# Local and global attention feeding a two-matrix feed-forward: maxima moved behind other VectorE work, low words moved to GpSimd

## The chip, the cores and the metric

One core of a Trainium2 chip. The metric is device microseconds of one execution, as the median of several runs; lower is better. The engines are PE (TensorE, matmuls), DVE (VectorE), ACT (ScalarE), POOL (GpSimd) and SP (which issues the DMAs). Each engine works through its own instructions in order; an instruction whose input is not ready holds back all that stand behind it on that engine.

## What is computed

```
k_all, v_all = concat(k_g, k_l), concat(v_g, v_l)      # batch 8, heads 8, 32 global + 512 local, depth 64
out_g = softmax(scale * q_g @ k_all.T) @ v_all
s_l   = concat(scale * q_l @ k_g.T, where(|i - j| <= 32, scale * q_l @ k_l.T, -1e9))
out_l = softmax(s_l) @ v_all
x = concat(out_g, out_l) as (4352 tokens, 512)
h = x @ w_in                                           # 512 x 2048
out = (h * cos(h)) @ w_out                             # 2048 x 512
```

Inputs and output are float32. w_in and w_out arrive as 64-bit words.

## The kernel before, in words

Matmuls run in 16-bit pairs: a float32 operand is split into a high plane and a low plane (float16), and three products (high x high, high x low, low x high) are summed. To split, an operand is first scaled by a power of two, which takes its maximum: of v for each batch (`v_a`), of w_in (`w_in_max`, `w_in_max_done`, `w_in_done`) and of w_out (`w_out_max`, `w_out_done`).

**Attention** runs in 32 groups: 8 batches b, two halves h of the queries, two groups g of two head pairs p. For a pair and half, `sc_a` computes scores (L549), `sc_b` adds the mask and takes the row minimum of the negated scores on DVE (L602), `sc_c` takes Exp on ACT (L437), `sc_d` normalizes into planes (L656, L657), `sc_e` transposes them (L679 by DMA, in the first half by PE and copies), `av_a` multiplies with the planes of v (L721), `av_b` scales the result by `xs` into x's high plane on ACT (L743) and low plane on DVE (L744). `g_a` and `g_b` compute the global queries' scores (L763, from batch 3 on L772) and minima (L785). `load_v` brings v of a batch into one buffer (L453); `v_a` takes its maximum on DVE (L488), `v_d` makes its planes.

**Feed-forward** runs in 17 chunks of 256 tokens (two to a batch; the last holds the global tokens) of 8 steps j. `m1_a` multiplies x with two 128-column blocks of w_in into a PSUM tile `ph` of three (L896); `m1_b` reduces the phase on ACT and DVE (L919, L920), `m1_c` takes Sin on ACT (L437), `m1_d` forms gf on DVE (L936), its high plane gh on ACT (L940) and low plane gl on POOL (L247); gf frees `ph`. `m2_a` multiplies gh, gl with w_out three steps later (L966). Exp and Sin need different ACT tables; `table_act` keeps them in the order in which they are written.

**Weights.** w_in comes in 8 blocks k (pair kc = k // 2, even or odd half of the columns): `w_in_load`, `w_in_max` (L280 on DVE), and `w_in_piece`: `decode` scales the high words on ACT (L261), makes the low words on DVE (L262) and joins both on DVE (L266); `split_w` casts to the high plane on ACT (L273), and POOL subtracts for the low plane (L247). Odd blocks lie raw in the tile that later holds w_out's planes, `wo_hl`. `xs`, the scale of x, needs the maxima of all of w_in. w_out comes in 16 blocks: each is loaded once for its maximum (`w_out_max`: the load at L406 and the reduction at L280 in one step, in borrowed room named by `ROOM`), and once more for its decoding (`w_out_load` for the first eight, or inside `w_out_piece`). `w_out_done` turns the maxima into the scale `wsc`.

**Order.** `at(slot, phase, f, ...)` writes the steps into slots, by hand; a step of the feed-forward takes slot 8c + j, and an attention group n has its parts at fixed distances from slot t = 4n + T0. Each step gets a priority from `pr` (or its own slot and phase), and a scheduler with a timeline simulation orders the instructions of each engine by priority among those that are ready in it. `behind(ins, what)` adds an order without a semaphore: the instruction is placed behind another. Line L1073 ff. set w_in's and w_out's steps, L1085 ff. the groups:

```
at(WOE + k // WOS, PJ, w_out_max, k, pr=(WO + k // WOS, PI))
...
at(-9, PB, w_out_done, pr=(WO + 7, PI))
...
t = 4 * n + T0
```

Of the kernel before, what the change touches and what calls it, by code (L numbers as in the profile page):

```python
# [49 lines left out]
LGC = 2  # L50
ROOM = "hlhlrrqqhlhlrrqq"
GB = 4
# [22 lines left out]
SW = 256  # L75
LO = "m01v456789:;"
JA = [None, "xl3", None, "xl3", None, "xl3", None, "xl3"]
# [69 lines left out]
def body(tc, qf, v, wi, wo, mask, out):  # L147
# [3 lines left out]
    with ExitStack() as ctx:  # L151
# [25 lines left out]

        wi_h = cp.tile([P, NPAIR, DF], F16, name="wi_h")
        wi_l = cp.tile([P, NPAIR, DF], F16, name="wi_l")
        wo_hl = cp.tile([P, NJ, 2, DM], F16, name="wo_hl")  # L180
# [76 lines left out]

        def decode(y, raw, s, low_after=None, join_after=None):
# [12 lines left out]

        def split_w(h, l, z, on_vector=False, cast="A", n=SPLIT):
            {"A": nc.scalar.copy, "D": nc.vector.tensor_copy, "G": nc.gpsimd.tensor_copy}[cast](h, z)  # L273
            if on_vector:
                nc.vector.tensor_tensor(l, z, h, op=ALU.subtract)
            else:
                pool_tt(l, z, h, ALU.subtract, n)

        def raw_max(o, raw):
# [45 lines left out]
        def w_in_max(k):  # L325
# [5 lines left out]
            if k % 2:  # L331
                m = wim[:, kc : kc + 1]
                nc.vector.tensor_reduce(m, wfs["s", kc], axis=AX.X, op=ALU.max)
                s = w1.tile([P, 1], F32, tag="ws", name=f"ws_{kc}", bufs=2)
# [61 lines left out]

        def w_out_max(j):
            room = ROOM[j]
            if room == "r":
                raw = w2.tile([P, 1024], U32, tag="raw", name=f"raw_wm{j}")  # L400
            elif room == "q":
                raw = ap_.tile([P, 2 * QK], U32, tag="qkr", name=f"raw_wm{j}", bufs=KQB)[:, :1024]
            else:
                t = ap_.tile([P, NPAIR, SL], F16, tag="x" + room, name=f"raw_wm{j}")
                raw = t.rearrange("p a b -> p (a b)").bitcast(U32)
            ld = nc.sync.dma_start(raw.bitcast(I64), wo[j * P : (j + 1) * P])  # L406
            maxes["wo", j] = raw_max(wos[:, j : j + 1], raw)

        def w_out_piece(j):
            if j < 8:  # L410
                raw = wo_raw[:, j]
# [64 lines left out]
        def v_a(b):  # L476
# [111 lines left out]
        def sc_b(b, p, i):  # L588
# [12 lines left out]
            for h in range(2):  # L601
                nc.vector.tensor_tensor_reduce(  # L602
                    t[:, h], pt[h], msk[:, MOFF[i] : MOFF[i] + w], nal, 3.0e38,
                    ALU.add, ALU.min, mn[:, h : h + 1],
                )
            st["t", b, p, i] = (t, mn)

        def sc_c(b, p, i):
# [6 lines left out]
            for h in range(2):  # L615
                table_act(
                    "Exp", t[:, h], t[:, h], AF.Exp, bias=mn[:, h : h + 1], scale=-1.0,
                    accum_out=sm[:, k + h : k + h + 1],
                )

        def sc_r(rr):
# [3 lines left out]
        def sc_d(b, p, i):  # L625
# [25 lines left out]
            else:  # L651
                for h in range(2):
# [81 lines left out]
        def av_b(b, hf, p):  # L734
            if (hf, p) == (0, 0):
                st["x", b] = (
                    ap_.tile([P, NPAIR, SL], F16, tag="xh", name=f"xh_{b}"),
                    ap_.tile([P, NPAIR, SL], F16, tag="xl", name=f"xl_{b}"),
                )
            xh, xl = (x[:, p, hf * CT : hf * CT + CT] for x in st["x", b])  # L740
# [144 lines left out]
        def m1_a(c, j, part=None):  # L885
# [6 lines left out]
            for a, kc in todo:  # L892
                f = slice((2 * j + a) * P, (2 * j + a + 1) * P)
                first, last = (a, kc) == (0, 0), (a, kc) == (1, NPAIR - 1)
                for ip, (w, x) in enumerate(((wi_h, xh), (wi_h, xl), (wi_l, xh))):
                    nc.tensor.matmul(  # L896
                        ph[:, a], w[:, kc, f], x[:, kc, q],
                        start=first and ip == 0, stop=last and ip == 2, skip_group_check=True,
# [31 lines left out]
        def m1_d(c, j):  # L930
            w = st.pop(("u", c, j))[1]
            n = w.shape[-1]
            gh = mp.tile([P, n], F16, tag="gh", name=f"gh_{c}_{j}", bufs=GB)
            gl = mp.tile([P, n], F16, tag="gl", name=f"gl_{c}_{j}", bufs=GB)
            gf = gf_tile(c, j, n)
# [274 lines left out]
```

## Time and profile before

| what | value |
|---|---|
| median of 3 runs | 947.88 us (945.82 to 949.18) |
| profiled execution, its own time | 949.29 us |
| its span, first to last instruction | 947.5 us |
| mean granted TensorE clock | 0.98 of full speed |
| PE busy | 881.5 us (93%) |
| ACT busy | 716.4 us (76%) |
| DVE busy | 649.5 us (69%) |
| POOL busy | 324.7 us (34%) |
| DMA moved | 104.88 MB, 111 GB/s on average |

The profile is of one execution; its own time is the span and 1.79 us around it. Times in the rows are microseconds from the start of the span. A matmul's record can overlap the one before it, since matmuls are pipelined, so that a busy PE is not PE at its peak. An engine's idle time costs nothing where another engine sets the pace.

### The profile page before, as it was taken

What the parts mean: (1) busy time and instruction counts of PE and PEld (TensorE: products, weight loads), DVE (VectorE), ACT (ScalarE), POOL (GpSimd) and SP (SyncE); (2) the same over time, 40 slices, a digit from 0 to 9 for tenths busy, and PEclk for the clock granted to TensorE, in tenths of its full rate; (3) what the DMA queues carried; (4) which work ended last, traced back from release to release, by engine and by line L of the source; (5) the groups of instructions that cost most, each with busy time, mean ns of one, the idle gap of its engine ahead of it and who ended that gap; (6) DMA issues with size and microseconds to landing.
All of it is one profiled execution on the core that took longest, in us unless ns stands there. A gap on an engine that the chain in (4) does not pass through costs nothing.

```text
span 947.5 us, 21219 instructions
## 1 busy us (share of the span) xinstructions
PE 881.5 (93%) x8055; PEld 594.9 (63%) x8055; DVE 649.5 (69%) x1757; ACT 716.4 (76%) x1472; POOL 324.7 (34%) x670
## 2 busy tenths in 40 slices
PE   5558899999999998999799998999899999999998
PEld 3446565566666665666566665666566676666676
DVE  5998879356766867687677867786777866764321
ACT  6948988678678886888588876898688788875442
POOL 5874556233323221223223322322132422333232
PEclk9997999999999999999899998999999999999999
DMA  9978565254435444433434464454334322430000
GB/s 383 403 268 262 99 169 145 69 107 82 130 75 111 89 105 113 93 92 76 130 62 103 80 148 79 89 98 83 113 75 110 60 68 46 82 59 24 1 24 23
DMA packets 164519, 104.88 MB, mean 111 GB/s; under 512 B 149568, under 2 KB 149952, under 8 KB 162368
## 3 DMA queue, kind: packets, MB, share of 16 engines
q1 hardware_dynamic: 164416, 103.52, 43.1%
q8 instruction: 63, 1.03, 0.5%
q14 instruction: 40, 0.33, 0.1%
HBM read 57.88 MB, written 8.91 MB: 70 GB/s over the span
## 4 chain that ended last, share of the span: by engine, by line
PE 39%; ACT 25%; DVE 24%; DMA 6%; issue 5%; POOL 1%; SPq 0%; ACTq 0%; DVEq 0%; POOLq 0%
PE po L966 18%; PE ph L896 17%; ACT t L437 5%; ACT L437 4%; ACT planes L656 4%; DMA vr<-v 4%; DVE t L602 3%; DVE u L920 3%; ACT w L437 3%; DVE qkr L584 3%; ACT u L919 3%; ACT qh L583 2%; DVE planes L657 2%; PE ps L549 2%; DVE vm L488 2%
## 5 line engine op out<-in xcount | busy, mean ns | idle before, releaser
L247 POOL TENSOR_TENSOR gl<-gf,gh 128x128 f16<-128x128 f32 x544 | 233.6, 463 | 469.7 <-ACT gh L940 431.4
L966 PE MATMUL po<-wo_hl,gh 128*128 128x512 f16 (+1 forms) x1120 | 322.7, 374 | 6.2 <-POOL wo_hl L247 6.2
L896 PE MATMUL ph<-xh,wi_h 128*128 128x256 f16 x1024 | 283.4, 278 | 6.9 <-ACT xh L743 5.2
L896 PE MATMUL ph<-xl,wi_h 128*128 128x256 f16 x1024 | 282.5, 277 | 1.4 <-DVE xl L744 1.4
L896 PE MATMUL ph<-xh,wi_l 128*128 128x256 f16 x1024 | 282.2, 277 | 0.0
L896 PEld LDWEIGHTS <-wi_h 128*128 128x128 f16 x2176 | 209.7, 99 | 54.5 <-issue 18.3
L966 PE MATMUL po<-wo_hl,gl 128*128 128x512 f16 (+1 forms) x560 | 204.6, 375 | 0.0
L966 PEld LDWEIGHTS <-gh 128*128 128x128 f16 x1120 | 109.9, 98 | 101.0 <-issue 2.2
L936 DVE SCALAR_TENSOR_TENSOR gf<-w,ph 128x512 f32<-128x512 f32 x136 | 93.2, 686 | 98.9 <-ACT w L437 97.0
L437 ACT ACTIVATE w<-u,pvs_hp,cs 128x512 f32<-128x512 f32 x136 | 109.9, 812 | 55.1 <-DVE u L920 53.6
L437 ACT ACTIVATE t<-t,mn 128x192 f32<-128x192 f32 (+1 forms) x256 | 116.6, 456 | 35.8 <-DVE mn L602 35.2
L920 DVE SCALAR_TENSOR_TENSOR u<-u,cs,ph 128x512 f32<-128x512 int32 x136 | 101.1, 745 | 58.0 <-ACT u L919 57.9
L919 ACT ACTIVATE u<-ph,pvs_hp,cs 128x512 int32<-128x512 f32 x136 | 104.6, 770 | 26.3 <-PE ph L896 26.3
L896 PEld LDWEIGHTS <-wi_l 128*128 128x128 f16 x1088 | 108.1, 99 | 17.1 <-issue 2.3
L940 ACT CAST gh<-gf 128x512 f16<-128x512 f32 x136 | 83.0, 611 | 37.6 <-DVE gf L936 33.1
L966 PEld LDWEIGHTS <-gl 128*128 128x128 f16 x560 | 54.9, 98 | 68.3 <-issue 7.4
L657 DVE SCALAR_TENSOR_TENSOR planes<-t,sm,planes 128x224 f16<-128x224 f32 (+1 forms) x244 | 93.9, 448 | 0.0
L656 ACT ACTIVATE planes<-t,sm 128x224 f16<-128x224 f32 (+1 forms) x244 | 90.8, 453 | 0.0
L437 ACT ACT_TABLE_LOAD x60 | 77.0, 1283 | 1.8 <-PEq L1200 0.7
L602 DVE CUSTOM_DVE_ANT_0 t<-ps,msk,qs 128x192 f32<-128x192 f32 (+1 forms) x160 | 59.7, 429 | 0.0
L721 PE MATMUL acc<-pt,vh 128*64 128x128 f16 (+2 forms) x896 | 45.7, 227 | 14.4 <-ACT vh L518 4.7
L721 PEld LDWEIGHTS <-vh 128*64 128x64 f16 x896 | 37.5, 113 | 28.9 <-issue 22.9
(176 smaller groups left out, 1066.1 us busy)
## 6 DMA issues: line engine op xcount, KB each, us to landing
qkr<-qf SPq DMA_DIRECT2D x32, 672.0 KB, 4.0
vr<-v SPq DMA_DIRECT2D x8, 1280.0 KB, 6.6
out<-o SPq DMA_DIRECT2D x33, 256.0 KB, 2.5
raw_wm<-wo SPq DMA_DIRECT2D x16, 512.0 KB, 9.8
raw_wi<-wi SPq DMA_DIRECT2D x4, 1024.0 KB, 16.7
wo_hl<-wi SPq DMA_DIRECT2D x4, 1024.0 KB, 18.5
wo_hl<-wo SPq DMA_DIRECT2D x8, 512.0 KB, 6.8
raw_wo<-wo SPq DMA_DIRECT2D x8, 512.0 KB, 4.9
```

The lines of the kernel that those rows point to most:

```text
L247: nc.gpsimd.tensor_tensor(o[..., c], a[..., c], b[..., c], op=op)
L437: ins = nc.scalar.activation(*a, **k).ins
L602: nc.vector.tensor_tensor_reduce(t[:, h], pt[h], msk[:, MOFF[i] : MOFF[i] + w], nal, 3.0e38, ALU.add, ALU.min, mn[:, h : h + 1],)
L656: a = nc.scalar.activation(hi, t[:, h], AF.Identity, scale=r)
L657: d = nc.vector.scalar_tensor_tensor(lo, t[:, h], r, hi, op0=ALU.mult, op1=ALU.subtract)
L721: mm = nc.tensor.matmul(acc[64 * h : 64 * h + 64, q_out : q_out + n0 * len(segs)], vt[:, tl, 64 * h : 64 * h + 64], rhs, start=(k == 0 and ...
L896: nc.tensor.matmul(ph[:, a], w[:, kc, f], x[:, kc, q], start=first and ip == 0, stop=last and ip == 2, skip_group_check=True,)
L919: nc.scalar.activation(k, ph, AF.Identity, scale=st["cs", c][4], bias=quarter)
L920: nc.vector.scalar_tensor_tensor(u, k, m, ph, op0=ALU.mult, op1=ALU.subtract)
L936: nc.vector.scalar_tensor_tensor(gf, w, -0.5, st.pop(("ph", c, j)).rearrange("p a b -> p (a b)"), op0=ALU.mult, op1=ALU.mult,)
L940: nc.scalar.copy(gh, gf)
L966: mm = nc.tensor.matmul(po[n], g[:, a * CT + k * P : a * CT + (k + 1) * P], w[:, 2 * j + a, c0:c1], start=(j == 0 and i == 0), stop=(j == ...
```

## The change

- The maximum of v (batch 1 and later) is placed behind the last score minimum written before it.
- `w_out_max` is divided: `w_out_room` loads a block into borrowed room, `w_out_max` reduces it. Blocks 0 to 11 are loaded right behind the opening's other loads, 12 and 13 at slot -9, 14 and 15 once 8 and 9 have been read. The rooms: both `raw` tiles, two `qkr` buffers, the two buffers each of x's planes, the second halves of `wi_h` and `wi_l` (blocks 8 to 11, then 14 and 15), two `pt` tiles. Maxima 4 and 5 are placed behind `xs`, the other fourteen behind x's low plane of the first half (`xl3`). Blocks 0 to 3 stay and are decoded where they are, without a second load.
- The low words of odd w_in blocks and of all w_out blocks are made by POOL, with a float multiply and add that rounds in place of shift and or.
- `wi_h` and `wi_l` are laid out in two halves by columns. Scaling of odd w_in blocks is placed behind the cast of block 6.
- The scores' operands of batch 0's second half are loaded in the opening (`LO`); its first group runs three slots earlier (`EARLY`); its Exp (i = 2) is placed behind x's high plane `xh3`.
- In chunk 0, gh and gl of steps 4 to 7 lie in batch 1's x tiles, which are taken with batch 0's. The order of the low score planes behind `dx` is gone.

```
+EARLY = {2: 3}
+PLW = "DGDGDGDG"
+PLO = "GGGGGGGGGGGGGGGG"
-ROOM = "hlhlrrqqhlhlrrqq"
+ROOM = "rrqqhlhl0123pp01"
-LO = "m01v456789:;"
+LO = "m01v456789:;23"
...
-            nc.scalar.activation(y, hi, AF.Prelu, scale=s, alpha=2.0**32)
-            low = nc.vector.tensor_scalar(
-                lo, lo, 29, 1, op0=ALU.logical_shift_right, op1=ALU.bitwise_or
-            )
+            p = nc.scalar.activation(y, hi, AF.Prelu, scale=s, alpha=2.0**32)
+            behind(p.ins, scale_after)
+            if pool_low:
+                low = nc.gpsimd.tensor_scalar(lo, lo, 2.0**-29, -0.53125, op0=ALU.mult, op1=ALU.add)
+            else:
+                low = nc.vector.tensor_scalar(
+                    lo, lo, 29, 1, op0=ALU.logical_shift_right, op1=ALU.bitwise_or
+                )
...
-            decode(z, raw, wfs["s", kc], join_after=JA[k])
-            c = slice(k % 2 * 1024, k % 2 * 1024 + 1024)
-            split_w(wi_h[:, kc, c], wi_l[:, kc, c], z, n=WIS)
+            decode(z, raw, wfs["s", kc], join_after=JA[k], pool_low=PLW[k] == "G",
+                   scale_after="cast6" if k % 2 else None)
+            cast = split_w(wi_h[:, k % 2, kc], wi_l[:, k % 2, kc], z, n=WIS)
+            if k == 6:
+                st["cast6"] = cast
...
-            ld = nc.sync.dma_start(raw.bitcast(I64), wo[j * P : (j + 1) * P])
-            maxes["wo", j] = raw_max(wos[:, j : j + 1], raw)
+            elif room == "p":
+                t = ap_.tile([P, 2, 8, P], F16, tag="pt", name=f"raw_wm{j}", bufs=2)
+                raw = t.rearrange("p a b c -> p (a b c)").bitcast(U32)
...
+                w = (wi_h, wi_l)[int(room) // 2][:, 1].rearrange("p a b -> p (a b)").bitcast(U32)
+                raw = w[:, int(room) % 2 * 1024 : int(room) % 2 * 1024 + 1024]
+            nc.sync.dma_start(raw.bitcast(I64), wo[j * P : (j + 1) * P])
+            st["wm", j] = raw
+
+        def w_out_max(j, after):
+            behind(raw_max(wos[:, j : j + 1], st["wm", j]), after)
...
-            if j < 8:
+            if j < 4:
+                raw = st.pop(("wm", j))
+            elif j < 8:
...
+            decode(z, raw, wsc, low_after="wsc", pool_low=PLO[j] == "G")
...
-                nc.vector.tensor_reduce(
+                vm = nc.vector.tensor_reduce(
                     m, st["vr", b], axis=AX.XYZ, op=ALU.max, apply_absolute_value=True
                 )
+                behind(vm.ins, "mn", "scores_first")
...
-                nc.vector.tensor_tensor_reduce(
+                st["mn"] = nc.vector.tensor_tensor_reduce(
...
+                if b == 0 and i == 2:
+                    behind(e, XB)
...
-                    if first and p == 3:
-                        behind(d.ins, "dx")
...
+            if c == 0 and GX <= j < GX + 4:
+                gh, gl = (x.rearrange("p a b -> p (a b)")[:, (j - GX) * n : (j - GX) * n + n] for x in st["x", 1])
...
-        for k in range(16):
-            at(WOE + k // WOS, PJ, w_out_max, k, pr=(WO + k // WOS, PI))
-            if k < 8:
-                at(ODD[k // 2], PK, w_out_load, k)
-        at(-9, PB, w_out_done, pr=(WO + 7, PI))
+        for j in range(14):
+            at(-23 if j < 12 else -9, PJ, w_out_room, j)
+            if j in (4, 5):
+                at(-11, PK, w_out_max, j, "xs")
+        for j in (8, 9, 6, 7, 10, 11, 0, 1, 2, 3, 12, 13, 14, 15):
+            at(-5, PI, w_out_max, j, "xl3", pr=(-6, PJ))
+            if j in (8, 9):
+                at(-5, PI, w_out_room, j + 6)
+        for j in range(4, 8):
+            at(ODD[j // 2], PK, w_out_load, j)
+        at(-5, PK, w_out_done, pr=(-6, PK))
...
-            t = 4 * n + T0
+            t = 4 * n + T0 - EARLY.get(n, 0)
```

## Rows read from the trace of the kernel before

**Rows 1.** Busy time by stretch (us; busy per engine and instructions; clock; DMA).

```profile
0.00:57.00 57.00, 27.81 (x235) 20.40 (x236) 46.62 (x148) 41.87 (x90) 39.40 (x64) 1.00 0.96 388
57.00:90.00 33.00, 27.06 (x161) 20.30 (x161) 31.10 (x92) 23.56 (x49) 16.61 (x24) 0.79 0.74 257
90.00:160.00 70.00, 61.29 (x576) 40.30 (x576) 58.63 (x146) 63.49 (x135) 39.96 (x65) 0.98 0.55 136
160.00:947.50 787.50, 765.31 (x7086) 513.89 (x7083) 513.12 (x1376) 587.47 (x1200) 228.77 (x518) 0.99 0.38 82
```

**Rows 2.** PE's waits from 160 us on (us in total, times, longest us).

```profile
PE gps L772 <- DVE mn L602: 16.2, 4, 5.5
PE ph L896 <- DVE xl L744: 0.9, 2, 0.6
PE gps L763 <- DVE mn L602: 0.8, 1, 0.8
```

**Rows 3.** Timeline of DVE, 464 us (start, duration; in brackets idle before, releaser).

```profile
464.14 2.82 DVE L488 TENSOR_REDUCE vm<-vr 128x1 f32<-128x2560 f32 x1 [5.59 <-DMA vr<-v]
466.88 0.41 DVE L602 CUSTOM_DVE_ANT_0 t<-ps,msk,qs 128x192 f32<-128x192 f32 x1
```

**Rows 4.** Timeline of PE at the same place.

```profile
468.43 0.43 PE L772 MATMUL gps<-qh 128*32 128x288 f16 x4 [5.49 <-DVE mn L602]
```

**Rows 5.** Busy time by stretch, around four stops of PE.

```profile
362.80:368.00 5.20, 5.20 (x39) 3.56 (x39) 4.59 (x12) 3.14 (x9) 0.00 (x0) 0.67 0.39 132
456.00:470.00 14.00, 8.51 (x107) 5.67 (x104) 8.19 (x16) 7.12 (x21) 1.86 (x5) 0.83 0.42 132
560.00:575.00 15.00, 11.23 (x125) 7.18 (x124) 10.81 (x27) 8.89 (x24) 3.53 (x8) 0.87 0.43 132
664.00:682.00 18.00, 14.18 (x145) 9.37 (x144) 13.16 (x35) 11.48 (x26) 3.75 (x8) 0.91 0.47 146
```

**Rows 6.** Timeline of DVE, opening.

```profile
58.52 0.86 DVE L744 SCALAR_TENSOR_TENSOR xl<-acc,xs,xh 128x256 f16<-128x256 f32 x2
...
64.43 2.81 DVE L488 TENSOR_REDUCE vm<-vr 128x1 f32<-128x2560 f32 x1
...
72.25 0.38 DVE L602 CUSTOM_DVE_ANT_0 t<-ps,msk 128x224 f32<-128x224 f32 x1
```

**Rows 7.** DVE's groups, 36 to 57.65 us (busy us, mean ns | idle before).

```profile
L280 DVE TENSOR_REDUCE wos<-raw_wm 128x1 f32<-128x512 f32 x13 | 8.5, 671 | 0.0
```

**Rows 8.** DVE's groups by shape, 0 to 160 us.

```profile
L262 DVE TENSOR_SCALAR wo_hl<-wo_hl 128x512 uint32<-128x512 uint32 x8 | 4.3, 532 | 0.0
...
L262 DVE TENSOR_SCALAR wo_hl<-wo_hl 128x1024 uint32<-128x1024 uint32 x4 | 3.3, 834 | 0.0
```

**Rows 9.** Timeline of ACT, opening.

```profile
61.14 4.55 ACT L273 CAST wi_h<-wo_hl 128x1024 f16<-128x1024 f32 x4 [2.74 <-DVE wo_hl L266]
...
79.33 0.81 ACT L437 ACTIVATE w<-u,pvs_hp,cs 128x512 f32<-128x512 f32 x1
```

**Rows 10.** Timeline of POOL.

```profile
62.41 12.11 POOL L247 TENSOR_TENSOR wi_l<-wo_hl,wi_h 128x256 f16<-128x256 f32 x16 [7.00 <-ACT wi_h L273]
...
156.78 1.31 POOL L247 TENSOR_TENSOR wo_hl<-z_wo,wo_hl 128x256 f16<-128x256 f32 x2 [1.98 <-DVE wo_hl L273]
```

**Rows 11.** Timeline of PE, first chunk.

```profile
81.31 0.37 PE L896 MATMUL ph<-xh,wi_h 128*128 128x256 f16 x1 [1.38 <-DVE gf L936]
...
86.39 0.31 PE L896 MATMUL ph<-xh,wi_h 128*128 128x256 f16 x1
...
90.56 0.38 PE L966 MATMUL po<-wo_hl,gh 128*128 128x512 f16 x1 [1.36 <-POOL wo_hl L247]
```

**Rows 12.** POOL's groups by shape, 0 to 160 us.

```profile
L247 POOL TENSOR_TENSOR wo_hl<-z_wo,wo_hl 128x256 f16<-128x256 f32 x32 | 22.9, 738 | 23.5 <-ACT wo_hl L273 13.6 <-DVE wo_hl L273 9.9
L247 POOL TENSOR_TENSOR gl<-gf,gh 128x128 f16<-128x128 f32 x40 | 21.9, 579 | 15.7 <-ACT gh L940 10.6 <-issue 5.1
...
L185 POOL CAST ident<-ident 128x128 f16<-128x128 f32 x1 | 0.3, 297 | 0.0
```

More of the change, by code (lines that the diff above doesn't have):

```diff
@@ L50 @@
 LGC = 2
-ROOM = "hlhlrrqqhlhlrrqq"
+XB = 'xh3'
+EL = 1
+GX = 4
+EARLY = {2: 3}
+PLW = "DGDGDGDG"
+PLO = "GGGGGGGGGGGGGGGG"
+ROOM = "rrqqhlhl0123pp01"
 GB = 4
@@ L176, in body @@
         nc.gpsimd.memset(planes_g, 0.0)
-        wi_h = cp.tile([P, NPAIR, DF], F16, name="wi_h")
-        wi_l = cp.tile([P, NPAIR, DF], F16, name="wi_l")
+        wi_h = cp.tile([P, 2, NPAIR, DF // 2], F16, name="wi_h")
+        wi_l = cp.tile([P, 2, NPAIR, DF // 2], F16, name="wi_l")
         wo_hl = cp.tile([P, NJ, 2, DM], F16, name="wo_hl")
@@ L272, in split_w @@
         def split_w(h, l, z, on_vector=False, cast="A", n=SPLIT):
-            {"A": nc.scalar.copy, "D": nc.vector.tensor_copy, "G": nc.gpsimd.tensor_copy}[cast](h, z)
+            c = {"A": nc.scalar.copy, "D": nc.vector.tensor_copy, "G": nc.gpsimd.tensor_copy}[cast](h, z)
             if on_vector:
@@ L277, in split_w @@
                 pool_tt(l, z, h, ALU.subtract, n)
+            return c.ins
         def raw_max(o, raw):
@@ L333, in w_in_max @@
                 nc.vector.tensor_reduce(m, wfs["s", kc], axis=AX.X, op=ALU.max)
-                s = w1.tile([P, 1], F32, tag="ws", name=f"ws_{kc}", bufs=2)
+                s = w1.tile([P, 1], F32, tag="ws", name=f"ws_{kc}", bufs=4)
                 mw = w1.tile([P, 1], F32, tag="wm43", name=f"wm43_{kc}", bufs=1)
@@ L395, in w_out_load, with w_out_room @@
             nc.sync.dma_start(wo_raw[:, j].bitcast(I64), wo[j * P : (j + 1) * P])
-        def w_out_max(j):
+        def w_out_room(j):
             room = ROOM[j]
@@ L402, in w_out_max @@
                 raw = ap_.tile([P, 2 * QK], U32, tag="qkr", name=f"raw_wm{j}", bufs=KQB)[:, :1024]
-            else:
+            elif room == "p":
+                t = ap_.tile([P, 2, 8, P], F16, tag="pt", name=f"raw_wm{j}", bufs=2)
+                raw = t.rearrange("p a b c -> p (a b c)").bitcast(U32)
+            elif room in "hl":
                 t = ap_.tile([P, NPAIR, SL], F16, tag="x" + room, name=f"raw_wm{j}")
                 raw = t.rearrange("p a b -> p (a b)").bitcast(U32)
-            ld = nc.sync.dma_start(raw.bitcast(I64), wo[j * P : (j + 1) * P])
-            maxes["wo", j] = raw_max(wos[:, j : j + 1], raw)
+            else:
+                w = (wi_h, wi_l)[int(room) // 2][:, 1].rearrange("p a b -> p (a b)").bitcast(U32)
[4 more added lines that the diff above has]
+            behind(raw_max(wos[:, j : j + 1], st["wm", j]), after)
         def w_out_piece(j):
-            if j < 8:
+            if j < 4:
+                raw = st.pop(("wm", j))
+            elif j < 8:
                 raw = wo_raw[:, j]
@@ L601, in sc_b @@
             for h in range(2):
-                nc.vector.tensor_tensor_reduce(
+                st["mn"] = nc.vector.tensor_tensor_reduce(
                     t[:, h], pt[h], msk[:, MOFF[i] : MOFF[i] + w], nal, 3.0e38,
                     ALU.add, ALU.min, mn[:, h : h + 1],
-                )
+                ).ins
             st["t", b, p, i] = (t, mn)
@@ L615, in sc_c @@
             for h in range(2):
-                table_act(
+                e = table_act(
                     "Exp", t[:, h], t[:, h], AF.Exp, bias=mn[:, h : h + 1], scale=-1.0,
@@ L734, in av_b @@
         def av_b(b, hf, p):
[L735 to L739, printed above, removed]
+            if (hf, p) == (0, 0) and b != 1:
+                for k in range(b, max(b, 1) + 1):
+                    st["x", k] = (
+                        ap_.tile([P, NPAIR, SL], F16, tag="xh", name=f"xh_{k}"),
+                        ap_.tile([P, NPAIR, SL], F16, tag="xl", name=f"xl_{k}"),
+                    )
             xh, xl = (x[:, p, hf * CT : hf * CT + CT] for x in st["x", b])
@@ L892, in m1_a @@
             for a, kc in todo:
-                f = slice((2 * j + a) * P, (2 * j + a + 1) * P)
+                t = 2 * j + a
+                f = slice(t % 8 * P, t % 8 * P + P)
                 first, last = (a, kc) == (0, 0), (a, kc) == (1, NPAIR - 1)
@@ L896, in m1_a @@
                     nc.tensor.matmul(
-                        ph[:, a], w[:, kc, f], x[:, kc, q],
+                        ph[:, a], w[:, t // 8, kc, f], x[:, kc, q],
                         start=first and ip == 0, stop=last and ip == 2, skip_group_check=True,
@@ L932, in m1_d @@
             n = w.shape[-1]
-            gh = mp.tile([P, n], F16, tag="gh", name=f"gh_{c}_{j}", bufs=GB)
-            gl = mp.tile([P, n], F16, tag="gl", name=f"gl_{c}_{j}", bufs=GB)
+            if c == 0 and GX <= j < GX + 4:
+                gh, gl = (x.rearrange("p a b -> p (a b)")[:, (j - GX) * n : (j - GX) * n + n] for x in st["x", 1])
+            else:
+                gh = mp.tile([P, n], F16, tag="gh", name=f"gh_{c}_{j}", bufs=GB)
+                gl = mp.tile([P, n], F16, tag="gl", name=f"gl_{c}_{j}", bufs=GB)
             gf = gf_tile(c, j, n)
@@ L1014, in attn @@
             first = (b, h, g) < (0, 1, 0)
-            if not first:
+            if b or h and not EL:
                 at(o["load"], PJ, load_qk, b, h, g)
@@ L1063, in body @@
                 at(-24, i, load_v, 0)
-            elif e < "2":
-                at(-24, i, load_qk, 0, 0, int(e))
+            elif e < "4":
+                at(-24, i, load_qk, 0, int(e) // 2, int(e) % 2)
             else:
```

3 lines of the change are left out of this document (1 added, 2 removed).

## The prediction, made before the changed kernel was run

> **What bounds the kernel now.** I read first the busy time by stretch, then the waits of PE, then the instructions around the longest of those waits, and last the groups of the opening. The stretches [rows 1] show two different kernels. From 160 us on PE is busy 765.3 of 787.5 us, so whatever delays PE there, or lets that stretch begin later, is paid one for one at the end. Before 160 us PE is the engine that waits: 29.2 of the first 57 us, 5.9 of the next 33, 8.7 of the next 70, while DVE is busy 46.6, 31.1 and 58.6 us in the same stretches and ACT 63.5 of the last 70.
>
> The waits [rows 2] name one cause for nearly all that PE loses late: the global scores (L772) waited four times, 16.2 us in all, for DVE's score minima (L602). The DVE rows show why [rows 3]: DVE stood still 5.59 us until the load of v had landed, then ran the maximum of v (L488, 2.82 us), and the four ready score minima were queued behind it, at 466.88. PE resumes 5.49 us late [rows 4]. After each such stop the granted clock is low [rows 5]: 0.67 over the 5.2 us after the one at 359.5, which is a mix of the two levels, 1.2 and 2.4 GHz.
>
> **The change, part by part.** *(a) Maximum of v behind the score minima.* The four minima go first and need nothing but finished score matmuls; the DMA wait then falls behind them. PE's four waits go: −16.2 us (a fifth of the same kind, 0.8 us, I leave in). The low clock that follows goes too. Lost there is (1 − granted) x length: 0.33 x 5.2 = 1.7, 0.17 x 14 = 2.4, 0.13 x 15 = 2.0, 0.09 x 18 = 1.6, together 7.7 us [rows 5]. What is late next? Behind the waiting maximum now stand only things that stood behind it anyway, first the u of the products (L920), which came after the minima and will now follow the maximum directly, four minima (some 1.5 us) sooner. Apart from the score minima PE's waits from 160 us on are of 0.9 us and less [rows 2], so nothing else is close behind, and I charge nothing. The bounds: 0, if some new wait of that length takes its place, to −23.9 us. I take −23.9, since the minima's own input was ready and nothing else in the rows holds PE. For v of batch 1 the same order puts 2.82 us [rows 6] behind both groups of second-half minima; v's planes are written three slots after the maximum, so I charge nothing for that move; it clears DVE's opening.
>
> *(b) w_out's maxima behind x's low plane.* Thirteen of the sixteen ran on DVE between 36 and 57.65 us, 8.5 us [rows 7], before the four low planes of x, the last of which starts at 58.52 [rows 6] and releases the first products. Two (blocks 4 and 5) may still come ahead, so 11/13 x 8.5 = 7.2 us leaves the path. The low words of the four odd w_in blocks leave DVE as well: 4 x 0.834 = 3.3 us [rows 8]. DVE had no gap there (the idle column of these groups is 0.0), so x's low plane can be ready some 10 us earlier, at 49. ACT does not hold it back: the odd blocks' four scalings are ordered behind the last even cast and fall into ACT's wait for xs. On GpSimd the four odd low words are worth some 4 x 2 us (price in (d)); it stood idle 7.0 us before its odd low planes [rows 10], which covers most; if they came ahead of an even low plane instead, x's products would wait by up to those 8 us, and the part gains 2 instead of 10.
>
> *(c) What the move pushes back.* Fourteen maxima now stand behind the low plane: 14 x 0.65 = 9.1 us. Blocks 8 to 11, 14 and 15 sit in the second halves of wi_h and wi_l, so the casts of the odd blocks wait for the very last of these maxima, and block 14 and 15 can only be loaded once 8 and 9 are read. From 49: 9.1 us of maxima and some 2.5 us of joins and minima between give about 61 us; before, the odd casts started at 61.1 [rows 9]. GpSimd then has its odd low planes, 12.1 us from 62.41 to 74.5 [rows 10]: unchanged. So products of the second half of w_in can't start before about 74 us. Before, the fourth product step started at 81.31 and waited for a buffer that the Sin chain frees (Sin at 79.33) [rows 9, 11], and the fifth at 86.39. This Sin chain moves earlier by more than 10 us, because the second-half scores are loaded and computed early (their loads move ahead of w_out's on SP), their Exp is ordered right behind x's high plane, and neither the maximum of v nor the joins stand ahead of the minima (72.25 before [rows 6]). The fifth step gains up to 86.4 − 74 = 12 us.
>
> *(d) Low words of w_out on GpSimd.* Sixteen of 512 columns leave DVE (0.53 us each [rows 8]) for GpSimd, whose trace has no such instruction. Bounds: memory writes and casts are its only one-operand rows; the 128-column cast takes 0.297 us [rows 12], four times that is 1.2; the two-operand subtraction takes 0.738 us for 256 columns, so 1.5 for 512 from above, and 0.5 (DVE's own) from below. I take 1.0, nearer to the one-operand row. First w_out pair ready: GpSimd free at 74.5, then 2 x (1.0 + 2 x 0.738) = 5.0 us, and 2.3 us of gl (4 x 0.579 [rows 12]), so 81.8 against 90.56 for the first m2 [rows 11]: −8.8 us. Per step of chunk 0 GpSimd then needs 2.3 + 5.0 = 7.3 us against (158.1 − 90.56)/8 = 8.4 us that a step took [rows 10, 11], so it does not become the bound. The Trainium skill (GPSIMD Engine Reference, section "Performance versus the Vector engine") speaks against this part: elementwise work belongs on VectorE, with 769 ns measured for a tight one-input loop over 512 elements; no row here shows it. By it the pair would take 4.5 us instead of 5.0 and the sum stays the same.
>
> Four w_out blocks are not read a second time (2 MB); the queue was hidden there.
>
> The stage gains the least of its three limits (10, 12, 8.8): **−9 us**.
>
> **Sum.** The profiled execution took 949.3 us (span 947.5): 949.3 − 23.9 − 9 = 916.4. The median of the runs shown is 1.4 us lower, so the changed kernel's should be about 915.
>
> **Rivals.** *R1, the opening gains nothing:* odd casts wait longer for blocks 14 and 15, or ACT (63.5 of 70 us busy) binds instead. Against: ACT idles in the first 57 us for 15 us that now get filled. 949.3 − 1.4 − 23.9 = 924. Chance 0.20. *R2, the order does not do what it says late:* the wait for v only moves onto u and Sin, and half of (a) comes back; or the minima were not ready. 949.3 − 1.4 − 12 − 9 = 927. For: u waits for the same load. Against: u comes sooner than before, not later. Chance 0.10. *R3, slower:* GpSimd's integer-to-float low word costs far more than any row suggests, and w_out's planes come late. With p us for each, chunk 0 takes 8 x (2.3 + 2p + 3.0) after 75; it ends at 158 for p = 2.6, and eats all of (a) as well from p = 4.1 on. At p = 5.5 it would be 949.3 + (75 + 130 − 158) − 24, less the 1.4, about 971. Chance 0.05. Its general form is the skill's rule named above, that GpSimd is the wrong place for elementwise work. *R4, the opening gains about twice as much:* PE's idle time and low clock between 57 and 160 us (14.6 us idle, and 0.21 x 33 = 6.9 us of clock [rows 1]) partly close too, as the second-half score matmuls move into PE's idle first 57 us: with 19 for 9, 905. Chance 0.20.
>
> **How the numbers follow.** My forecast, 915, gets 0.43; the rivals 0.20, 0.10, 0.05 and 0.20; 0.02 is left for a change that nearly cancels. The range runs from 901 (R4 and a little beyond) to 930 (R1, R2). 0.3% is 2.8 us, about what a measurement of this kernel can tell from no change: faster 0.92, same 0.02, slower 0.06.
>
> **What would show it.** Right: PE's waits have no global scores behind the score minima; each late maximum of v stands behind four minima; x's last low plane starts near 49 us, the fifth product step near 74, the first m2 near 82; from 160 us on the clock is 1.00 throughout. Wrong: u (L920) or ACT's Sin in place of the minima as PE's releaser; GpSimd busy without gaps from 75 us to the last w_out piece; the odd casts still open at 66 us; a low word on GpSimd of more than 2.6 us.

## The result, and the profile after

The changed kernel took 924.38 us (median of 4 runs, 923.92 to 926.0) beside 948.12 us (945.82 to 949.18) for the kernel before: ratio 0.9756, 95% interval 0.9734 to 0.9778, so 23.7 us faster. The range 901 to 930 held it; the forecast, 915, was 9 us too low. The time is the one that rival R1 (the opening gains nothing) gave, 924, though not for quite its reasons, as the marks below show. The profiled execution took 926.0 us, span 924.2.

In the changed kernel the code has moved: L602 became L627 (score minima), L488 L512 (maximum of v), L280 L291 (the other maxima), L262 L270 on GpSimd and L272 on DVE (low words), L266 L276 (joins), L273 L283 (casts), L744 L770 (x's low plane), L896 L923, L966 L996, L763 L789, L772 L798, L982 L1012, L437 L461 (Exp and Sin), L247 L253 (subtractions on GpSimd), L936 L966 (gf), L211 L217 (a maximum's broadcast on PE). In the experiments made from it the lines lie up to four further down, or one up (e1); e2 has the lines of the kernel before, one further down.

First the busy time by stretch of the changed kernel, as in [rows 1].

```profile
0.00:57.00 57.00, 32.84 (x269) 23.95 (x270) 44.74 (x160) 46.30 (x108) 42.68 (x68) 0.77 0.94 376
57.00:90.00 33.00, 23.32 (x196) 16.43 (x194) 26.39 (x69) 23.83 (x50) 18.02 (x30) 0.72 0.67 181
90.00:160.00 70.00, 61.06 (x507) 38.79 (x506) 52.73 (x136) 59.55 (x122) 49.57 (x79) 0.93 0.56 152
160.00:924.20 764.20, 758.26 (x7090) 510.13 (x7090) 512.00 (x1376) 585.86 (x1197) 226.12 (x514) 1.00 0.38 85
```

From 160 us on PE is busy 758.3 of 764.2 us, idle 5.9, at a clock of 1.00; before it was idle 22.2 of 787.5 at 0.99 [rows 1]. The first 160 us look quite different: PE is no busier than before in all (117.2 us against 116.2, the sums of the first three rows), at a lower clock. Next PE's waits from 160 us on, which answer to [rows 2] (total, times, longest).

```profile
PE ph L923 <- DVE xl L770: 1.7, 5, 0.4
```

That row, 1.7 us, is all that is left; the global scores do not wait for score minima any more. The timelines of DVE and PE at the places that answer to [rows 3] and [rows 4]:

```profile
502.31 0.41 DVE L627 CUSTOM_DVE_ANT_0 t<-ps,msk,qs 128x192 f32<-128x192 f32 x1
...
502.72 2.81 DVE L512 TENSOR_REDUCE vm<-vr 128x1 f32<-128x2560 f32 x1
```

```profile
456.74 0.31 PE L798 MATMUL gps<-qh 128*32 128x288 f16 x4
```

The maximum of v has four minima before it, as predicted, and no bracket: DVE did not wait for the data, which had landed. It does not stand at 464 us, though, but two groups later. The other late ones start at 302.51, 403.12, 602.32 and 701.92, all without idle time, against 256.28, 358.51, 568.18 and 673.14 before, each of which had waited 3.45 to 4.07 us for its load. The global scores at the former stop start without a wait.

Then the opening, which answers to [rows 6, 9, 10 and 11]: DVE, ACT, PE and POOL.

```profile
53.78 0.87 DVE L770 SCALAR_TENSOR_TENSOR xl<-acc,xs,xh 128x256 f16<-128x256 f32 x2
54.56 1.27 DVE L291 TENSOR_REDUCE wos<-wi_h 128x1 f32<-128x512 f32 x2
...
67.74 0.68 DVE L291 TENSOR_REDUCE wos<-wi_h 128x1 f32<-128x512 f32 x1
...
68.69 0.68 DVE L291 TENSOR_REDUCE wos<-wi_h 128x1 f32<-128x512 f32 x1
...
72.13 0.33 DVE L209 TENSOR_SCALAR d_wo<-ident,wm_o 128x128 bf16<-128x128 f32 x1
```

```profile
70.25 4.14 ACT L283 CAST wi_h<-wo_hl 128x1024 f16<-128x1024 f32 x4
...
77.74 1.52 ACT L461 ACTIVATE w<-u,pvs_hp,cs 128x512 f32<-128x512 f32 x2
```

```profile
72.51 0.26 PE L217 MATMUL pm_wo<-d_wo,ones 128*128 128x128 bf16 x1 [8.67 <-DVE d_wo L209]
...
89.30 0.28 PE L923 MATMUL ph<-xh,wi_h 128*128 128x256 f16 x1
...
93.29 0.38 PE L996 MATMUL po<-wo_hl,gh 128*128 128x512 f16 x1 [0.21 <-POOL wo_hl L253]
```

```profile
71.41 7.88 POOL L253 TENSOR_TENSOR wi_l<-wo_hl,wi_h 128x256 f16<-128x256 f32 x12 [16.18 <-ACT wi_h L283]
79.38 3.21 POOL L270 TENSOR_SCALAR raw_wm<-raw_wm 128x512 uint32<-128x512 uint32 x4
...
154.46 1.30 POOL L253 TENSOR_TENSOR wo_hl<-z_wo,wo_hl 128x256 f16<-128x256 f32 x2 [1.09 <-DVE wo_hl L283]
```

x's low plane is 4.7 us sooner (53.78 for 58.52; each row holds the last two of four parts, and the last part starts at 54.17 for 58.91). Fourteen maxima follow it, the last at 68.69, and the odd casts start at 70.25 instead of 61.14. GpSimd waits 16.18 us for them, the fourth product step starts at 81.60 as it did before (81.31), the fifth 2.9 us *later* (89.30 for 86.39), and the first product with w_out is 2.7 us *later* (93.29 for 90.56). The end of w_out's decoding is 2.3 us sooner (154.46 for 156.78).

How far this carries is seen in PE's waits between 57 and 160 us, of the kernel before and then of the changed one (rows of 0.5 us and less left out):

```profile
PE po L966 <- POOL wo_hl L247: 6.2, 4, 2.3
PE ph L896 <- ACT xh L743: 4.9, 1, 4.9
PE acc L721 <- DMA pt<-planes: 2.9, 3, 2.0
PE pm_wo L211 <- DVE d_wo L203: 2.7, 1, 2.7
PE ph L896 <- DVE gf L936: 1.6, 2, 1.4
```

```profile
PE po L996 <- POOL wo_hl L253: 8.7, 4, 4.6
PE pm_wo L217 <- DVE d_wo L209: 8.7, 1, 8.7
```

With the small rows the sums are 19.3 and 18.4 us, but the first wait for x's plane ended at 57.36, so that 4.5 of the 19.3 us lie before 57 us. By the busy times above and in [rows 1], PE's idle time was 29.2 us before and 24.2 after in the first 57 us, 14.6 and 18.6 from there to 160 us: 43.8 and 42.8 together. **The opening's waits changed their names and places, not their length.** The largest new one is PE's: the small matmul that broadcasts w_out's maximum (`pm_wo`) stood in PE's order for 8.67 us until the last maximum was done, with all else queued behind it.

The same is read from the marks of the chunks, which are counted from 1 here (chunk 2 follows what the prediction calls chunk 0): the start of DVE's scaling of the second output tile of a chunk (`o<-po`), here in us for before, after, and three experiments of the next section.

| chunk | before | after | after, v free (e1) | only the order (e2) | v behind the nearer minima (e3) |
|---|---|---|---|---|---|
| 2 | 200.26 | 199.01 | 201.33 | 200.33 | 197.86 |
| 6 | 405.72 | 400.07 | 406.59 | 401.42 | 399.12 |
| 10 | 616.38 | 599.26 | 617.09 | 600.62 | 601.14 |
| 13 | 772.80 | 749.78 | 773.50 | 751.15 | 755.19 |
| 17 | 942.33 | 919.29 | 943.02 | 920.68 | 924.73 |

Of the 23.0 us at the last mark 1.3 are there at chunk 2; the rest comes up to chunk 13, in steps at the places where PE stopped before. The 1.3 us compare two executions at different clocks: in the first 57 us 1.00 was granted before and 0.77 after. A second profile of the unaltered changed kernel (e9 below), with 0.94 there, has its chunk 2 mark at 197.02, so the opening's gain is 1.3 to 3.2 us.

### The profile page after: what moved, and what is told of

Same layout as the page of the kernel before. It is cut to its first block, busy times and chain, and to the rows that moved or that the text cites. A ratio compares the mean times of both kernels' runs of the same rounds, so it can differ in the third digit from the quotient of the medians.

```text
span 924.2 us, 21213 instructions
## 1 busy us (share of the span) xinstructions
PE 875.5 (95%) x8055; PEld 589.3 (64%) x8055; DVE 635.9 (69%) x1737; ACT 715.5 (77%) x1472; POOL 336.4 (36%) x690
## 4 chain that ended last, share of the span: by engine, by line
PE 59%; ACT 17%; DVE 14%; issue 4%; POOL 3%; DMA 2%; SPq 0%; DVEq 0%; ACTq 0%; POOLq 0%
PE po L996 26%; PE ph L923 25%; ACT t L461 4%; PE ps L574 3%; ACT L461 3%; ACT w L461 3%; DVE u L947 2%; PE acc L746 2%; ACT planes L683 2%; DVE t L627 2%; DVE qkr L609 2%; ACT u L946 2%; ACT qh L608 1%; DMA raw_wi<-wi 1%; POOL wi_l L253 1%
## 5 line engine op out<-in xcount | busy, mean ns | idle before, releaser
L253 POOL TENSOR_TENSOR gl<-gf,gh 128x128 f16<-128x128 f32 x528 | 222.3, 452 | 443.5 <-ACT gh L970 423.6
L996 PE MATMUL po<-wo_hl,gh 128*128 128x512 f16 (+1 forms) x1088 | 314.3, 374 | 4.2 <-POOL wo_hl L253 4.1
L923 PE MATMUL ph<-xl,wi_h 128*128 128x256 f16 x1024 | 279.9, 274 | 1.7 <-DVE xl L770 1.7
L923 PE MATMUL ph<-xh,wi_h 128*128 128x256 f16 x1024 | 279.9, 275 | 0.6
L923 PE MATMUL ph<-xh,wi_l 128*128 128x256 f16 x1024 | 279.1, 274 | 0.0
L923 PEld LDWEIGHTS <-wi_h 128*128 128x128 f16 x2176 | 206.9, 98 | 48.3 <-issue 14.1
L996 PE MATMUL po<-wo_hl,gl 128*128 128x512 f16 (+1 forms) x544 | 199.8, 374 | 0.0
L996 PEld LDWEIGHTS <-gh 128*128 128x128 f16 x1088 | 106.6, 98 | 96.4 <-issue 1.6
L966 DVE SCALAR_TENSOR_TENSOR gf<-w,ph 128x512 f32<-128x512 f32 x136 | 93.3, 686 | 107.2 <-ACT w L461 107.0
L461 ACT ACTIVATE w<-u,pvs_hp,cs 128x512 f32<-128x512 f32 x136 | 110.3, 813 | 58.2 <-DVE u L947 56.5
L461 ACT ACTIVATE t<-t,mn 128x192 f32<-128x192 f32 (+1 forms) x256 | 116.6, 458 | 6.1 <-DVE mn L627 5.8
L923 PEld LDWEIGHTS <-wi_l 128*128 128x128 f16 x1088 | 107.0, 98 | 18.1 <-issue 4.6
L970 ACT CAST gh<-gf 128x512 f16<-128x512 f32 x132 | 80.5, 610 | 38.5 <-DVE gf L966 30.3
L996 PEld LDWEIGHTS <-gl 128*128 128x128 f16 x544 | 53.4, 98 | 64.6 <-issue 5.3
L627 DVE CUSTOM_DVE_ANT_0 t<-ps,msk,qs 128x192 f32<-128x192 f32 (+1 forms) x160 | 59.7, 429 | 0.0
L769 ACT ACTIVATE xh<-acc,xs 128x256 f16<-128x256 f32 x64 | 29.4, 465 | 33.1 <-DVE xl L770 24.5
```

The source lines that it names most:

```text
L253: nc.gpsimd.tensor_tensor(o[..., c], a[..., c], b[..., c], op=op)
L461: ins = nc.scalar.activation(*a, **k).ins
L627: st["mn"] = nc.vector.tensor_tensor_reduce(t[:, h], pt[h], msk[:, MOFF[i] : MOFF[i] + w], nal, 3.0e38, ALU.add, ALU.min, mn[:, h : h + 1] ...
L923: nc.tensor.matmul(ph[:, a], w[:, t // 8, kc, f], x[:, kc, q], start=first and ip == 0, stop=last and ip == 2, skip_group_check=True,)
L966: nc.vector.scalar_tensor_tensor(gf, w, -0.5, st.pop(("ph", c, j)).rearrange("p a b -> p (a b)"), op0=ALU.mult, op1=ALU.mult,)
L970: nc.scalar.copy(gh, gf)
```

## The experiments

**e1: the order of v taken back.** Two theories had to be told apart: the late order alone pays, or the opening has a hidden share.

```
-                behind(vm.ins, "mn", "scores_first")
```

> The changed kernel with v's maximum free again (its order behind the score minima taken out, all else kept). Theory A: nearly the whole gain is this order; the marks of the finished chunks in the two traces part by 1 to 2 us in the opening and by 21 us at the v stops. Then this runs at 943 to 947 us and PE again waits some 16 us for minima in four places. Theory B: the opening's parts also feed the late stretch (buffers, loads): then 930 to 938.

Measured: 949.8 us, ratio 1.0005 (0.9993 to 1.0017), above both ranges, with theory A's four waits. All other parts of the change bring nothing without this order. (It was taken from batch 1's maximum too, whose 2.8 us go back into the opening: the chunk 2 mark is 2.3 us later than the changed kernel's.) PE's waits from 160 us on, and DVE at the stop:

```profile
PE gps L797 <- DVE mn L626: 16.4, 4, 5.5
```

```profile
465.15 2.82 DVE L512 TENSOR_REDUCE vm<-vr 128x1 f32<-128x2560 f32 x1 [5.44 <-DMA vr<-v]
467.89 0.41 DVE L626 CUSTOM_DVE_ANT_0 t<-ps,msk,qs 128x192 f32<-128x192 f32 x1
```

These are [rows 2] and [rows 3] again, with 16.4 for 16.2 us and 5.44 for 5.59. The Trainium skill (PSUM — Partial Sum Buffer, section "Engine vs sequencer instructions") calls the queue of VectorE strictly first in, first out; the trace agrees, the ready minimum stood 5.44 + 2.82 us behind one that was not ready.

**e2: only the order of v, in the kernel before.**

```
-                nc.vector.tensor_reduce(
+                vm = nc.vector.tensor_reduce(
...
+                behind(vm.ins, "mn", "scores_first")
...
-                nc.vector.tensor_tensor_reduce(
+                st["mn"] = nc.vector.tensor_tensor_reduce(
...
```

> The kernel before with nothing but v's maximum placed behind the last score minimum written before it. Theory A: 925 to 928 us, within 3 us of the changed kernel, PE's four waits gone. Theory B: 933 to 942. Should it be faster than the changed kernel, the opening's parts cost time.

Measured: 929.23 us, ratio 0.9787 (0.9766 to 0.9807), 1 us above theory A's range. This one order gives 0.0213 x 949 = 20.2 us. What the rest of the change adds to it is the step from 0.9787 to 0.9756, 2.9 us, with intervals that overlap; the profiled executions differ by 1.4 at the last mark. PE's waits from 160 us on:

```profile
PE ph L897 <- DVE xl L745: 1.8, 5, 0.4
```

**e3: the maximum behind the nearer minima.** The prediction had it at its old place, only behind the four minima that it used to hold up. The change puts it behind those that are *written* last before it, which run two groups later. Here it stands where the prediction had it.

```
-                behind(vm.ins, "mn", "scores_first")
+                behind(vm.ins, "mn" if b < 2 else ("mn", 4 * b - 3), "scores_first")
...
+            st["mn", 4 * b + 2 * hf + p // 2] = st["mn"]
```

> The changed kernel with v's maximum placed right behind the four minima it used to hold back (group 4b - 3), two groups sooner than the change places it; this is the place that my prediction took. If those four minima were all that mattered: 924 to 926 us, with DVE waiting some 2 us for v's load in each batch and PE waiting for nothing. Rival: scales, u and Sin behind the waiting maximum hold PE, 1 to 3 us in each of five batches: 929 to 938.

Measured: 930.78 us, ratio 0.9801 (0.9783 to 0.9819), 0.0045 x 949 = 4.3 us slower than the changed kernel and in the rival's range. DVE at the stop, then PE's waits from 160 us on:

```profile
456.42 2.82 DVE L512 TENSOR_REDUCE vm<-vr 128x1 f32<-128x2560 f32 x1 [1.07 <-DMA vr<-v]
```

```profile
PE ph L924 <- DVE xl L771: 4.0, 9, 0.6
PE ps L574 <- DVE mn L627: 1.3, 4, 0.4
PE ph L924 <- ACT xh L770: 0.8, 1, 0.8
```

The wait for the load is still there, 1.02 to 2.15 us at each of the five places (6.6 us in all), and PE's waits are 6.1 us where the changed kernel has 1.7. What releases PE is not u or Sin, as the rival had it, but x's planes and score minima. The marks show where: e3 is 1.2 us ahead of the changed kernel at chunk 2 and 5.4 behind it at the end, and loses a bit at each v. So most of the gain is in letting the minima pass, and the rest is in the distance: two groups later the load has landed. The move costs nothing at the other end, since no row of the changed kernel has PE waiting for v's planes.

**e4: the odd casts set free.** The casts waited for the second halves of `wi_h`, into which blocks 14 and 15 are loaded once 8 and 9 have been read there. Here these two go into the `pt` tiles, and the maxima of blocks 8 to 13 come first.

```
-ROOM = "rrqqhlhl0123pp01"
+ROOM = "rrqqhlhl0123pppp"
...
-        for j in (8, 9, 6, 7, 10, 11, 0, 1, 2, 3, 12, 13, 14, 15):
+        for j in (8, 9, 10, 11, 12, 13, 6, 7, 0, 1, 2, 3, 14, 15):
...
-            if j in (8, 9):
-                at(-5, PI, w_out_room, j + 6)
+            if j in (12, 13):
+                at(-5, PI, w_out_room, j + 2)
```

> The changed kernel with w_out's blocks 14 and 15 loaded for their maxima into the two pt tiles (behind blocks 12 and 13 there) and not into w_in's second half; maxima 8 to 13 come first. Theory O: the odd casts stand on ACT until the last maxima are read (70.3 us; Sin behind them at 77.7), and that ate the opening's gain. Then the odd casts start at 60 to 64, Sin near 70, and the time falls to 916 to 921 us. Rival P: w_out's scale and GpSimd's low planes set the opening: no change, 923 to 926. Rival Q: the transposes of the second half wait for the pt tiles: slower, 926 to 932.

Measured: 927.54 us, ratio 0.9767 (0.9747 to 0.9787): no gain. That is in rival Q's range, but PE has no wait for the `pt` tiles. The casts did start when the prediction had them, at 60.18, and w_out's last piece is done 6 us sooner (148.44). But the last maximum now runs at 73.99 instead of 68.69, so the broadcast comes later, and PE stands longer in front of it. ACT's first odd cast, then PE's waits from 57 to 160 us:

```profile
60.18 1.16 ACT L283 CAST wi_h<-wo_hl 128x1024 f16<-128x1024 f32 x1
```

```profile
PE pm_wo L217 <- DVE d_wo L209: 13.0, 1, 13.0
PE po L996 <- POOL wo_hl L253: 8.3, 6, 3.6
```

**e5 and e6: the broadcast moved behind the second half's global scores,** alone and together with e4. The first mends PE's wait, the two together mend both.

```
+            if name == "wo":
+                behind(mm.ins, "gps1", "scores_first")
...
-        at(-5, PK, w_out_done, pr=(-6, PK))
+        at(-4, PK, w_out_done, pr=(-6, PK))
```

> The changed kernel, with one matmul moved on PE: the spread of w_out's maxima (pm_wo, w_out_done a slot later) is placed behind the global scores of the second half. In the changed kernel PE stood 8.67 us at pm_wo, waiting for the last of the delayed maxima, with those scores behind it; their minima, their Exp, the table load and so the first Sin (77.7 us) came after. Theory H: this wait on PE is what holds the opening. Then the first Sin comes at 66 to 70 us and the time falls by 5 to 9 us, to 916 to 921. Rival O: the odd casts, still held by blocks 14 and 15, hold the next product steps anyway: 923 to 926.

> Both at once: blocks 14 and 15 in the pt tiles, and pm_wo behind the global scores. Theory H with O: odd casts at 60, first Sin at 66 to 70, and the time at 912 to 918. If only H counts: as the run without the other rooms. If GpSimd or w_out's scale sets the opening: 923 to 927.

Measured: 926.59 us (0.9765, 0.9739 to 0.979) and 925.29 us (0.9754, 0.9729 to 0.9779): no gain either. In e6 the odd casts start at 61.35 and Sin at 66.89, eleven us sooner than in the changed kernel, yet w_out's maximum is ready for PE only at 78.75 (72.13), and its broadcast runs at 83.13 (72.51). In e5 Sin comes at 66.46, as theory H had it, and the time stays. PE's waits of e6 from 57 to 160 us:

```profile
PE ph L927 <- DVE gf L970: 11.2, 5, 5.5
PE po L1000 <- POOL wo_hl L255: 4.3, 2, 2.7
PE acc L748 <- DMA pt<-planes: 3.2, 4, 0.9
```

The 8.7 us at `pm_wo` are gone, and 11.2 us stand in front of the products of the first steps, whose `ph` tiles come free only with gf.

**e7: fourteen maxima left out.** A bound for all that the maxima behind x's low plane can cost. This kernel computes w_out's scale from two blocks' maxima alone and leaves out the loads that served only the others.

```
+        nc.vector.memset(wos, 0.0)
...
-        for j in range(14):
+        for j in range(6):
...
-            at(-5, PI, w_out_max, j, "xl3", pr=(-6, PJ))
-            if j in (8, 9):
-                at(-5, PI, w_out_room, j + 6)
+            pass
```

> Leaves out work: w_out's scale is taken from blocks 4 and 5 alone; the other fourteen maxima and the loads that served only them are gone. It bounds what the place of the maxima can cost behind x's low plane. Theory: 9 us of DVE work and the waits for it (PE at pm_wo, odd casts) vanish, so 908 to 916. If the opening is bound by ACT and GpSimd all the same: 920 to 925.

Measured: 919.15 us, ratio 0.9683 (0.9657 to 0.9709), between the two ranges. ACT and PE in the opening:

```profile
57.02 3.26 ACT L283 CAST wi_h<-wo_hl 128x1024 f16<-128x1024 f32 x3
```

```profile
82.53 0.56 PE L997 MATMUL po<-wo_hl,gh 128*128 128x512 f16 x1 [2.68 <-POOL wo_hl L253]
```

With the odd casts at 57 the first product with w_out comes at 82.5, the place at which the prediction had it (81.8). Even so the chunk 2 mark moves only from 199.01 to 192.73, 6.3 us, although w_out's last piece is 11 us sooner (143.50). Beside e9, whose opening ran at a clock nearer to this one's (0.97 and 0.84 up to 90 us here, 0.94 and 0.74 in e9), it is 4.3 us. In time the fourteen maxima and their loads are worth 5 us (against e9's ratio) to 7 (against the first one).

**e8, e10 and e12: the low words of w_out back on DVE, twice, and shared between both engines; e9: the changed kernel again; e11: the low words on DVE with the rooms and the order of e6.**

```
-PLO = "GGGGGGGGGGGGGGGG"
+PLO = "DDDDDDDDDDDDDDDD"    # e8, e10, e11
+PLO = "GDGDGDGDGDGDGDGD"    # e12
```

> The changed kernel with the low words of all 16 w_out blocks back on DVE (the odd w_in ones stay on GpSimd). By the changed kernel's profile one costs GpSimd 0.64 to 0.80 us and it is not the bound: 922 to 927. If the load of GpSimd between 71 and 100 us is what delays the first w_out planes: faster, 918 to 921. If DVE misses the 8 us taken off it: 928 to 932.

> The changed kernel once more, unaltered, so that the three variants of this call stand beside it on the same chip. Both theories: about 924.5, ratio 0.975, and the spread of this run says which differences below it are none.

> All low words of w_out on DVE again, beside the changed kernel on the same chip. Theory (GpSimd's low words delay w_out's planes in chunk 0): 1 to 3 us below the changed kernel, as the earlier mark of chunk 2 (196.26 against 199.01) says. Rival (nothing, the earlier 1 us was spread): within 1 us of the changed kernel.

> Low words of w_out on DVE, and the other order of rooms with the scale's broadcast behind the global scores. Theory (w_out's planes hold chunk 0, so that each helps once the other is done): 920 to 922, the mark of chunk 2 near 194. Rival (DVE, with all low words and the joins, takes over as the bound): 924 or more, no gain over the low words alone.

> Low words of w_out shared, even blocks on GpSimd, odd blocks on DVE. Theory (GpSimd's work per step of chunk 0 holds w_out's planes): half of the gain of the low words on DVE, 0.5 to 1.5 us below the changed kernel. Rival (both engines are near their limit, so that sharing is best): more than all on DVE gives, 921 or less.

| run | us | ratio, 95% interval | chunk 2 mark |
|---|---|---|---|
| e8, by DVE | 923.45 | 0.973 (0.9709 to 0.9751) | 196.26 |
| e9, the changed kernel | 924.96 | 0.9737 (0.971 to 0.9763) | 197.02 |
| e10, by DVE again | 925.06 | 0.9735 (0.9709 to 0.9761) | 196.55 |
| e11, by DVE, and e6 | 928.14 | 0.9765 (0.9738 to 0.9792) | 200.83 |
| e12, shared | 927.67 | 0.9761 (0.9736 to 0.9787) | 199.50 |

e8 looked like 1 us and 2.75 at the mark; side by side on one chip the two kernels are 0.1 us apart, and the unaltered kernel moved its own mark by 2.0 us. The theory (GpSimd's low words delay chunk 0) does not explain the time: with the low words on DVE the first product with w_out does come 2.7 us sooner, but 0.5 us of it is left at the chunk 2 mark. That product in e9 and e10:

```profile
91.96 0.38 PE L996 MATMUL po<-wo_hl,gh 128*128 128x512 f16 x1 [0.21 <-POOL wo_hl L253]
```

```profile
89.27 0.59 PE L996 MATMUL po<-wo_hl,gh 128*128 128x512 f16 x2
```

And the windows from 90 to 160 us of e9 and of e10, where the figures after the length are PE, weight loads, DVE, ACT and GpSimd, each with its count:

```profile
90.00:160.00 70.00, 59.70 (x509) 38.37 (x507) 53.36 (x140) 60.53 (x122) 49.22 (x80) 0.98 0.56 151
```

```profile
90.00:160.00 70.00, 61.92 (x565) 40.81 (x564) 59.94 (x149) 62.43 (x128) 40.10 (x69) 0.98 0.63 160
```

Nine us of GpSimd became 6.6 of DVE; PE was busy 2.2 us more in this stretch, and the time shows none of it. So the rivals of e10 (no gain) and e11 (924 or more) held. The medians of e11 and e12 are 3.2 and 2.7 us above e9's, though the intervals of the ratios overlap; e12 is above both of its ranges, and why sharing loses was not settled. No version that does the same work beats the changed kernel clear of the spread; e2, the order alone, comes within some 3 us of it by the ratios.

## Why the prediction was right, and where not

**(a), the maximum of v: right in cause, near in size, wrong in place.** The sum gave 23.9 us, 16.2 of waits and 7.7 of clock. Between e1 and the changed kernel, which differ in this line alone, lie (1.0005 - 0.9756) x 949 = 23.6 us; in the kernel before the order gave 20.2. That 23.6 meets 23.9 so closely is in part luck: 2.3 us of it are there at the chunk 2 mark already, from batch 1's maximum in the opening. From chunk 2 to chunk 17 the marks gain 21.4 us between these two, 21.8 between the kernel before and the changed one, 21.7 with the order alone. PE's idle time from 160 us on fell by 16.3 us (22.2 to 5.9), as priced. That leaves some 5.5 us for the clock, which is 1.00 there now where [rows 5] had 0.67 to 0.91: the 7.7 of the sum was 2 us too much, and why was not settled. The step that failed is "the DMA wait then falls behind them": at the place where the prediction left the maximum that wait would have stayed, and e3 prices it at 4.3 us. "Behind the last score minimum written before it" was read as the nearest on the engine; written last and run last are not the same where steps of several groups are written into one slot. R2, which lets the wait move onto other work, had its mechanism right for e3, not for this kernel.

**(b), x's low plane 10 us sooner: it was 4.7.** The stretch from the end of the last maximum of w_in to x's first low plane did shrink, from 21.7 us (36.0 to 57.67) to 14.5 (38.3 to 52.81). But the last maximum of w_in began 2.3 us later than before (37.10 for 34.81), behind score planes of the first half that had come after it, and eight score minima of the early second half, from 47.16 to 50.09, now stand where maxima stood. The step took the place of the removed instructions as free; the same change had moved others into it.

**(c), the odd casts at 61: they came at 70.25.** This is the step that failed most. It added 9.1 us of maxima and 2.5 of joins to a start at 49. Of its 9 us error 5 come from (b); the rest is that four joins took 4.7 us and the first u (1.4) and the first planes came between. "The fifth step gains up to 12 us" fell with it: the fourth came no sooner and the fifth 2.9 us later. e4 and e7, where the casts start at 60.18 and 57.02, show that the maxima, by their order and their rooms, were the cause.

**(d), the low words on GpSimd: right in price, 1.0 estimated, no cost.** GpSimd's groups by shape, 0 to 160 us:

```profile
L270 POOL TENSOR_SCALAR wo_hl<-wo_hl 128x1024 uint32<-128x1024 uint32 x4 | 5.7, 1416 | 0.3
...
L270 POOL TENSOR_SCALAR raw_wo<-raw_wo 128x512 uint32<-128x512 uint32 x8 | 5.4, 678 | 2.9 <-DMA raw_wo<-wo 1.8 <-ACT gh L970 0.6
```

512 columns take 0.68 us here (0.67 and 0.74 in the other two groups), within the bounds 0.5 to 1.5. The Trainium skill's 769 ns (GPSIMD Engine Reference, section "Performance versus the Vector engine") is a little above it. The rule there that this work belongs on VectorE made no difference to the time: e10 and e9 are equal. Of the 11 us by which the first w_out product missed its place (93.29 for 82), some 3 go with these words (e10 beside e9); e7 has it at 82.53 with the words still on GpSimd, so that the maxima are the larger cause.

**"The stage gains the least of its three limits: -9 us."** The inputs of this step failed. Here are the three limits as the prediction had them, as the runs had them, and the chunk 2 mark (us):

| run | x's last low plane | fifth product step | first w_out product | chunk 2 mark |
|---|---|---|---|---|
| predicted | 49 | 74 | 82 | |
| before | 58.91 | 86.39 | 90.56 | 200.26 |
| after | 54.17 | 89.30 | 93.29 | 199.01 |
| e4 | 53.16 | 92.05 | 87.32 | 199.57 |
| e5 | 54.03 | 74.25 | 99.43 | 200.61 |
| e6 | 53.66 | 72.48 | 91.11 | 200.69 |
| e7 | 53.88 | 77.50 | 82.53 | 192.73 |

In the changed kernel only the first of the three came sooner than before. In e4, e5 and e6 one of the other two did, the fifth step even where the prediction had it, but the remaining one came later than before, and the mark stayed. Nor does an early first chunk carry: in e4 the mark of chunk 1 came at 153.63 for 164.57 before, and at chunk 2 0.7 us of that are left. The three share DVE's and PE's order, so that what one gains the next wait takes: PE's idle time in the first 160 us is 43.8 us before, 42.8 after and 45.2 in e6. Only in e7, without the fourteen maxima, do all three come sooner, and its mark is 7.5 us ahead of the kernel before. So the step that failed is the move of the maxima in (c): it charged them with their 9.1 us on DVE and counted what stands behind them, the casts and PE's broadcast, as unchanged, and this took 4.3 to 6.3 us of the 9 (e7, which leaves out their loads too). Whether the stage gains the least of three, no run tests.

R1 had the right time and, in its first half, the right cause (casts that wait for blocks 14 and 15), but e4 shows that this cause alone does not explain it. Its time is in part luck too: the opening did gain 1.3 to 3.2 us, and (a) gave 2 us less than its sum. What holds the rest of the opening was not settled.

R3 fell with the price of the low words, R4 with the opening's waits. Of the signs that the prediction named, the score minima, the maximum of v and the clock from 160 us on were as for right, and the odd casts still open at 66 us as for wrong.

## What to carry to other kernels

An engine's order is a resource of its own: an instruction that waits for a transfer is placed behind everything that is ready, and far enough behind that the transfer has landed; passing the ready work gave some 19 us here (e1 to e3), the distance another 4. Before an opening is rearranged, sum the idle time of the engine that sets the pace, and ask for each removed wait which one stands next in the same order; limits that share an in-order queue do not move one by one. Repeat the unaltered kernel beside a variant before a gain of a microsecond is believed.

## What was not expected of the hardware

The granted clock of the opening differs between executions of the same kernel: 0.77, 0.72 and 0.93 in the three stretches of the first profile, 0.94, 0.74 and 0.98 in the second (e9), with PE busy 117.2 and 115.9 us; the chunk 2 mark moved by 2.0 us with it. A low word of 1024 columns on GpSimd took 1.14 us at 18.23 and 1.96 at 38.57, beside a join on DVE, and 1.42 in the mean of four. And DVE's join of 1024 columns, 1.2 us each in the four of the opening's second part, took 2.06 at 28.08, beside such a low word, but 1.33 at 38.23 beside another; that the two engines slow each other down was not tested.
